# Local attention with a routed expert layer: two experts picked from batch 0's counts, three rounds written in line

## Chip, cores and metric

The kernel runs on one core of one Trainium2 chip. The metric is the device time of one execution in microseconds; lower is better. The five engines have their own instruction queues: TensorE (PE, with its weight loads as PEld), VectorE (DVE), ScalarE (ACT), GpSimd (POOL) and SyncE (SP, which here only issues DMAs and reads registers).

## Reference

Two parts follow one another. The first is attention over 2 batches, 8 heads, 768 positions and a head dimension of 64: each query sees the keys nearer than 16 positions, and besides them one key and one value for each block of 32 positions (the maximum of the block's keys, the mean of its values). The second part takes the result as 1536 rows of 512 numbers. Each row goes to the one of 8 experts whose logit is largest; an expert takes its first 384 rows and drops the others.

```python
k_sum = k.reshape(B, H, nb, block, D).max(axis=3)
v_sum = v.reshape(B, H, nb, block, D).mean(axis=3)
scores_l = np.where(np.abs(pos[:, None] - pos[None, :]) < 16, scale * (q @ k.T), -1e9)
scores_s = scale * (q @ k_sum.T) + np.log(block)
a = softmax(np.concatenate([scores_l, scores_s], axis=-1))
x = (a @ np.concatenate([v, v_sum], axis=2))      # 1536 rows of 512

logits = x @ w_gate                               # 8 experts
expert_idx = np.argmax(logits, axis=1)
gate_w = softmax(logits)[rows, expert_idx]
# the first 384 rows of each expert, in order, are disp[e]
h = np.maximum(np.einsum('ecd,edf->ecf', disp, w1), 0.0)   # F = 1024
y = np.einsum('ecf,efd->ecd', h, w2)
out[i] = gate_w[i] * y[expert_idx[i], pos[i]]              # 0 for dropped rows
```

The routing depends on the data. With these inputs batch 0 sends 363 rows to expert 0 and 405 to expert 7, and none to the others; both batches together send 504 to expert 0, 594 to expert 3 and 438 to expert 7. So three experts are in use, each is full, and expert 7 is full from batch 0 alone.

## The kernel before

**One order.** All work up to the end of the first expert round is a list of named steps, `SEQ`, which is run from left to right when the kernel is built. Each step appends its instructions to the queues of the engines that it uses, and each engine takes its queue in order. So a step's place in the list decides what stands ahead of it on its engine.

**Attention.** A chunk `c` (0 to 7) is two heads of one batch, a group `n` (0 to 23) four tiles of 64 queries. `k`, `q`, `t` and `v` load a chunk; `w`, `Q`, `kb`, `kp` and `vb`, `vt`, `vk`, `vp`, `vP` lay out keys, queries, block keys and block values. `kb` and `vb` are reductions on VectorE. Per group, `S` computes the scores (TensorE), `M` their maximum (VectorE), `E` the exponentials (ScalarE), `R` transposes them (TensorE), `K` copies them out of PSUM (ScalarE). `V` multiplies with the values (TensorE) and `N`, two steps on VectorE, divides by the sums; `V` of half `h` uses one PSUM buffer, which `N` of the half before sets free. Chunk 0 is prepared ahead of the list.

**Routing.** For each batch `x`, `X`, `l`, `L`, `g` compute the logits, `ch` and `ga` choose the expert and the gate's weight, and `ga` ends with a store of the batch's 768 rows to HBM (`xrow`). `pf` counts, `pl` places each row, and a census (`tk`) turns this by small matmuls into a table of row numbers by expert. `ts1` adds the tables of both batches (the tile `tid`).

**Rounds.** A round handles one expert with at most 384 rows. It loads w1 and w2 in four parts each (`lw`, `lW`) on SP's queue, gathers three tiles of 128 rows by indirect DMA (`fr`, POOL), transposes them (`T`, TensorE), and splits rows and weights into a high and a low part of fewer mantissa bits: `H` and `h1`, `h2` on ScalarE, `I` and `s1`, `s2` on VectorE. `u` is one eighth of the first layer (12 matmuls), `r` and `e` its relu and the low part of that; `D` is the second layer for one tile of rows (24 matmuls), after which the tile is weighted (tile `y`, ScalarE) and put to its rows in `out` by an indirect DMA on POOL.

Round 0 is picked from batch 0 alone: `pick` takes the expert with the most rows there, `first` reads its number into a register of SP, and its steps up to its first down tile (`D0`) stand in `SEQ`, between the routing steps of batch 1. The chain `rd` (the function `rounds`) then sorts the experts that are left by count, on VectorE. After the list the number of rounds left (`nr`) is read on all engines and the eight expert numbers on SP, and `tower` nests the other rounds in branches: within `If(nr > r)` the next round's loads and splits are interleaved with the down tiles of the round before; the `Else` finishes the last round.

Of the kernel before, what the change touches and what calls it, by code (L numbers as in the profile page):

```python
# [22 lines left out]
P = 128  # L23
# [89 lines left out]
q1 k1 S0 q3 z2 k2 M0 S1 t0 Q11a E0 M1 Q10p R0 kb1 E1 w1p q2 S2 K0 R1 kp1p k3 Q31a M2 Q30p v0 K1 S3 E2 kb2 w2p t1 R2 M3 S4 K2 vb0 kp2p E3 z3 R3 t3 M4  # L113
Q21a v1 vt0 S5 vk0 Q20p E4 kb3 R4 vp0 K3 M5 S6 vP0 E5 R5 w3p M6 E6 S7 kp3p vb1 misc zr V00 t2 M7 K4 v2 V01 N00 E7 N00 vt1 N01 q6 S8 N01 vk1 vb3 K5 vP1
S9 M8 t4 vp1 k4 R6 M9 E8 v3 R7 V10 K6 q4 vb2 K7 V11 k5 E9 N10 t5 N10 vt2 N11 S10 vk2 N11 vp2 vt3 vP2 S11 M10 vk3 Q61a vP3 R8 M11 E10 R9 vb4 V20 vp3 K8
Q60p K9 V21 N20 N20 E11 w4p q5 vt4 kb4 R10 t7 vk4 R11 K10 N21 v6 V30 N21 kp4p K11 v7 V31 N30 N30 x0 N31 k6 N31 Q40p Q41a x1 x2 X0a k7 X1a S12 w5p kb5
v5 X2a S13 M12 kp5p q7 vb5 E12 v4 vP4 l00 M13 t6 vp4 Q51a R12 E13 vt5 Q50p S14 vb7 vk5 R13 K12 vP5 M14 S15 L00a K13 vp5 E14 x3 M15 x4 X3a x5 X4a S16
X5a E15 g00 M16 R14 R15 E16 w6p kb6 S17 K14 K15 kp6p l01 kb7 w7p R16 L01a M17 S18 E17 kp7p g01 M18 R17 ch0 S19 E18 ch0 Q70p ch0 ch0 ch0 Q71a ch0 ch0
S20 M19 ch0 ga0 E19 ga0 pf0 ga0 pick ga0 M20 V40 pl0 K16 pick V41 pl0 pick vb6 K17 S21 pick pl0 pick pl0 pick pl0 pl0 pick pl0 vt6 pick R18 pl0 vk6
E20 R19 vP6 vt7 pl0 pl0 pl0 pl0 tk0 vk7 pick pick pick pick first lw0 lw1 M21 vp6 K18 S22 lw2 pads ts0 rows vP7 E21 N40 rows rows lw3 pads N40 R20  # L120
# [9 lines left out]
def attention_moe(ctx: ExitStack, tc: tile.TileContext, qT, kT, vT, vw, wg, w1, w2, cf, cm, cr, cv, out, cap: int):  # L130
# [121 lines left out]
    def key_blocks_put(c, eng):  # L252
        cast(eng, kt[c][:, :, WIN:KW], ksum[c].unsqueeze(1).to_broadcast([P, NT, NB]))
# [260 lines left out]
    class Round:  # L514
        def __init__(self, e, turn):
            self.e, self.turned, self.xp, self.hp, self.yp = e, turn, {}, {}, {}
# [114 lines left out]
        def down(self, j, tag=None):  # L631
            ps = psum.tile([P, DM], F32, tag=tag or f"av{j % 2}", name="yp", bufs=1)
            n = 0
            for f in range(KF):
                g, i = divmod(f, 2)
                for a, w in ((0, 0), (0, 1), (1, 0)):
                    nc.tensor.matmul(ps, self.h[g][:, i, a, P * j : P * j + P], self.w2[g][:, w, i, :], start=n == 0, stop=n == 3 * KF - 1)  # L637
                    n += 1
            self.yp[j] = ps

        def put(self, j):
            oid = small.tile([P, 1], I32, tag="oid", name="oid")
# [44 lines left out]
    sel, plans, ops = {}, [], {}  # L687
    ENGINES = {"p": nc.gpsimd, "a": nc.scalar, "v": nc.vector}
# [31 lines left out]
    def pick():  # L720
# [20 lines left out]
    def rows():  # L741
        sel["ids0"] = yield from places(tbs[0], sel["eq0"], 0, 1, "a")

    def rows_fetch(j):
        sel["R"].fetch_rows(sel["ids0"][:, 0], P * EARLY, j)

    def pads():
        eq0 = sel["eq0"][:, 0]
        mine = const.tile([P, E], F32, name="mine")
        c0 = const.tile([P, 1], F32, name="c0")  # L750
        nc.vector.tensor_tensor(out=mine, in0=sel["cl0"], in1=eq0, op=ALU.mult)
        yield
        nc.vector.tensor_reduce(out=c0, in_=mine, op=ALU.add, axis=AX.X)
        if nsub > 1:
            yield
            nc.vector.tensor_scalar(out=c0, in0=c0, scalar1=float(RW), scalar2=None, op0=ALU.min)
        sel["c0"] = c0
        yield
        pad = yield from padding(c0, 1, "a")
        sel["R"].pad = pad[:, 0]  # L760

    def rounds(s):
# [17 lines left out]
        cnt, k7, ei = yield from unpack(mx, E, f"b{s}")  # L780
# [50 lines left out]
    for r, R in enumerate(routes):  # L831
        for i in range(TPB):
            op(f"x{TPB * r + i}", R.turn, i)
            op_on(f"X{TPB * r + i}", R.take, i)
        for j in range(TPB // LB):
            op(f"l{r}{j}", R.logits, j)
            op_on(f"L{r}{j}", R.logits_keep, j)
            op(f"g{r}{j}", R.gather, j)
        chain(f"ch{r}", R.choose)
        op(f"pf{r}", R.prefix)  # L840
        chain(f"pl{r}", R.place)
        chain(f"ga{r}", R.gate)
# [119 lines left out]
```

## Time and profile before

| | |
|---|---|
| runs, us | 205.19, 207.51, 207.7; median 207.51 |
| profiled execution, us | 204.78 |
| its span, first to last instruction, us | 202.8 |
| mean granted TensorE clock | 0.967 of full speed |
| TensorE busy, us | 181.4 (89% of the span) |
| VectorE, ScalarE, GpSimd busy, us | 103.1, 103.1, 60.3 |
| DMA | 38.8 MB, mean 191 GB/s |

The span is the stretch that the trace covers; the profiled execution's own time is 2 us longer. All rows below are from this one execution, with times in us from the span's start. A granted clock of 1.00 is 2.4 GHz, one of 0.50 is 1.2 GHz. Attention ends at about 75 us, and the first round's products begin at 81.5.

### The profile page before, as it was taken

What the parts mean: (1) busy time and instruction counts of PE and PEld (TensorE: products, weight loads), DVE (VectorE), ACT (ScalarE), POOL (GpSimd) and SP (SyncE); (2) the same over time, 40 slices, a digit from 0 to 9 for tenths busy, and PEclk for the clock granted to TensorE, in tenths of its full rate; (3) what the DMA queues carried; (4) which work ended last, traced back from release to release, by engine and by line L of the source; (5) the groups of instructions that cost most, each with busy time, mean ns of one, the idle gap of its engine ahead of it and who ended that gap; (6) DMA issues with size and microseconds to landing.
All of it is one profiled execution on the core that took longest, in us unless ns stands there. A gap on an engine that the chain in (4) does not pass through costs nothing.

```text
span 202.8 us, 3980 instructions
## 1 busy us (share of the span) xinstructions
PE 181.4 (89%) x1461; PEld 159.5 (79%) x1461; DVE 103.1 (51%) x219; ACT 103.1 (51%) x227; POOL 60.3 (30%) x79
## 2 busy tenths in 40 slices
PE   7689999999996797999999349999998999989990
PEld 2577999989995595999988247999986899978870
DVE  3275697665599499836630760185470318520000
ACT  5568788789775699822101550473543146311100
POOL 6596638955416500000041020481012010000111
PEclk9889999999999999999999967999999999999996
DMA  6889599999858999803519999179001110000111
GB/s 201 273 294 324 112 319 320 363 269 265 200 205 252 360 383 403 325 2 117 199 52 300 360 377 352 68 236 366 21 0 52 52 53 5 2 10 3 52 55 52
DMA packets 20218, 38.80 MB, mean 191 GB/s; under 512 B 1450, under 2 KB 8284, under 8 KB 20188
## 3 DMA queue, kind: packets, MB, share of 16 engines
q1 hardware_dynamic: 18256, 33.43, 50.6%
q0 software_dynamic: 1440, 4.73, 6.6%
q10 hardware_dynamic: 492, 0.28, 0.7%
q8 instruction: 14, 0.23, 0.5%
q14 instruction: 16, 0.13, 0.2%
HBM read 29.77 MB, written 8.66 MB: 189 GB/s over the span
## 4 chain that ended last, share of the span: by engine, by line
PE 61%; DMA 10%; ACT 9%; issue 8%; DVE 7%; SPq 3%; POOL 1%; another core or an unknown queue 0%; POOLq 0%; DVEq 0%; ACTq 0%
PE hp L620 24%; PE yp L637 12%; PE sc L280 8%; PE pt L294 5%; PE av L308 5%; DMA w1r<-w 4%; DMA out<-y,oid 3%; DMA qc<-qT 2%; ACT prob L289 2%; PE xp L341 2%; ACT pts L298 2%; ACT w1h L227 1%; PE sc L281 1%; PE xgp L594 1%; PE lq L352 1%
## 5 line engine op out<-in xcount | busy, mean ns | idle before, releaser
L637 PE MATMUL yp<-w,h 128*128 128x512 f32 x216 | 52.4, 403 | 0.5 <-ACT h L625 0.5
L637 PEld LDWEIGHTS yp<-w,h 128*128 128x128 f32 x216 | 41.9, 196 | 9.6 <-issue 0.8
L620 PE MATMUL hp<-xh,w1h 128*128 128x384 f32 x96 | 32.7, 340 | 0.0
L620 PE MATMUL hp<-xh,w1l 128*128 128x384 f32 x96 | 32.2, 335 | 0.0
L620 PE MATMUL hp<-xl,w1h 128*128 128x384 f32 x96 | 32.1, 335 | 0.0
L646 POOL DMA_INDIRECT out<-y,oid x9 | 8.9, 994 | 76.9 <-ACT y L645 55.8
L289 ACT ACTIVATE prob<-sc,nm 128x120 f32<-128x120 f32 x96 | 27.0, 381 | 6.6 <-DVE nm L285 5.5
L280 PE MATMUL sc<-k,qb 128*128 128x120 f32 x192 | 26.9, 285 | 2.0 <-POOL qb L223 1.8
L280 PEld LDWEIGHTS sc<-k,qb 128*128 128x128 f32 x192 | 24.6, 200 | 3.6 <-POOL qb L223 2.1
L625 ACT ACTIVATE h<-hp 128x384 fp32r<-128x384 f32 x24 | 11.8, 492 | 29.6 <-PE hp L620 29.6
L285 DVE TENSOR_REDUCE nm<-sc 128x4 f32<-128x480 f32 x24 | 15.7, 656 | 17.6 <-PE sc L281 10.7
L629 DVE SCALAR_TENSOR_TENSOR h<-hp,h 128x384 fp32r<-128x384 f32 x24 | 13.3, 556 | 21.9 <-ACT h L625 21.8
L645 ACT ACTIVATE y<-yp,xgb 128x512 f32<-128x512 f32 x9 | 6.1, 687 | 33.2 <-PE yp L637 31.9
L575 DVE TENSOR_TENSOR w1l<-w1r,w1h 128x1024 fp32r<-128x1024 f32 x12 | 14.3, 1221 | 10.0 <-ACT w1h L227 10.0
L566 POOL DMA_INDIRECT xgb<-xrow,b0ids x6 | 8.6, 1426 | 35.5 <-DVE b0pad L494 34.0
L223 POOL TENSOR_SCALAR v<-vrow 25x520 f32<-25x520 f32 (+1 forms) x16 | 14.0, 874 | 15.8 <-ACT vrow L263 11.3
L620 PEld LDWEIGHTS hp<-xh,w1h 128*128 128x128 f32 x96 | 18.0, 188 | 0.3 <-issue 0.2
L620 PEld LDWEIGHTS hp<-xl,w1h 128*128 128x128 f32 x96 | 18.0, 188 | 0.1
L620 PEld LDWEIGHTS hp<-xh,w1l 128*128 128x128 f32 x96 | 18.0, 188 | 0.0
L227 ACT CAST w1h<-w1r 128x1024 fp32r<-128x1024 f32 x12 | 12.3, 1062 | 10.7 <-DMA w1r<-w 10.7
L294 PE MATMUL pt<-cft,prob 128*121 128x128 f32 x96 | 16.5, 301 | 0.9 <-ACT prob L289 0.7
L581 DVE TENSOR_TENSOR w<-w2r,w 128x1024 fp32r<-128x1024 f32 x12 | 14.6, 1226 | 3.9 <-ACT w L227 3.7
(116 smaller groups left out, 231.3 us busy)
## 6 DMA issues: line engine op xcount, KB each, us to landing
w1r<-w SPq DMA_DIRECT2D x12, 512.0 KB, 7.3
w2r<-w SPq DMA_DIRECT2D x12, 512.0 KB, 9.3
v<-vw SPq DMA_DIRECT2D x16, 292.5 KB, 7.2
kc<-kT SPq DMA_DIRECT2D x8, 400.0 KB, 6.1
xrow<-x SPq DMA_DIRECT2D x2, 1542.0 KB
vc<-vT SPq DMA_DIRECT2D x8, 384.0 KB, 4.6
out<-zrow SPq DMA_DIRECT2D x1, 3072.0 KB
qc<-qT SPq DMA_DIRECT2D x7, 384.0 KB, 7.0
```

Source lines behind the costliest of these rows:

```text
L223: eng.tensor_scalar(out=dst, in0=src, scalar1=f, scalar2=0.0, op0=ALU.mult, op1=ALU.add)
L227: nc.scalar.copy(out, in_)
L280: nc.tensor.matmul(self.sc[:, i, :], qb[c % NQ][:, t, :], kt[c][:, t, :], start=i == 0, stop=False)
L285: nc.vector.tensor_reduce(out=self.nm, in_=self.sc, op=ALU.max, axis=AX.X, negate=True)
L289: nc.scalar.activation(self.pr[:, i, :KW], self.sc[:, i], AF.Exp, bias=self.nm[:, i : i + 1])
L294: nc.tensor.transpose(self.pt[:KV, P * i : P * i + P], self.pr[:, i], ident)
L575: eng.tensor_tensor(out=self.w1l[g], in0=self.w1r[g], in1=self.w1h[g].bitcast(F32), op=ALU.subtract)
L581: eng.tensor_tensor(out=self.w2[g][:, 1], in0=self.w2r[g], in1=self.w2[g][:, 0].bitcast(F32), op=ALU.subtract)
L620: nc.tensor.matmul(ps, a[g][:, kk, fo : fo + P], x[:, kk, :], start=n == 0, stop=n == 3 * KD - 1)
L625: nc.scalar.activation(self.h[f // 2][:, f % 2, 0], self.hp[f], AF.Relu)
L629: nc.vector.scalar_tensor_tensor(out=h[:, f % 2, 1], in0=self.hp[f], scalar=0.0, in1=h[:, f % 2, 0].bitcast(F32), op0=ALU.max, op1=ALU.sub ...
L637: nc.tensor.matmul(ps, self.h[g][:, i, a, P * j : P * j + P], self.w2[g][:, w, i, :], start=n == 0, stop=n == 3 * KF - 1)
```

## The change

`pick` now takes the two experts with the most rows in batch 0. The first is round A, as before. The second is round B: its expert number is read from the same result (`firstB`), its rows and count come from the tables of both batches (`rowsB`, `padsB`). `rounds` removes both from the counts and sorts the others; the first of these is round C (`firstC`, `set`). All three rounds stand in `SEQ`, from loads to puts, without a branch; `down`, the row numbers of the output (`o`), the weighting (`y`) and the put (`P`) are steps of their own. `nr` is still read on all engines, and what is left after three rounds is done by a nest of branches at the end, a round at a time. `SEQ` is a new list throughout: the steps of attention and routing are the same but stand in another order. Ahead of the list, chunk 0's queries and block keys are laid out by other engines in other pieces.

The end of the list of before, from the last steps of the attention on:

```
h11a N61 K22 V70 s11v K23 V71 lW0 lW1 lW2 lW3 fill h12a N70 N70 x6 h13a s12v x7 X6a x8 s13v X7a X8a T0 N71 T1 N71 H0 l10 H1 I0 h20a I1 T2 L10a s20v H2
x9 h21a x10 I2 g10 X9a u0 s21v X10a h22a h23a s22v x11 u1 X11a s23v r0 e0 r1 l11 e1 u2 L11a g11 r2 u3 ch1 e2 ch1 ch1 ch1 ch1 ch1 ch1 u4 r3 ch1 e3 ga1
ga1 ga1 ga1 pf1 r4 cl1 u5 pl1 pl1 pl1 pl1 pl1 pl1 e4 pl1 pl1 u6 r5 pl1 pl1 pl1 pl1 e5 tk1 r6 u7 ts1 rd e6 rd rd rd rd rd rd r7 rd rd rd rd e7 D0 rd rd
rd rd rd rd rd rd rd rd rd rd rd
```

The diff, cut (of the new list the start, the stretch around pick, and the end):

```diff
@@ -110,19 +110,24 @@
+q1 k1 t0 S0 k2 z2 t2 S1 M0 q2 Q11a M1 Q10p E0 w1p q3 kb1 E1 S2 kp1p vb0 R0 z3 R1 M2 t1 K0 S3 K1 k3 kb2 E2 v0 w2p vt0 M3 v2 vk0 vb2 S4 kp2p E3 vP0 v1
...
+ch0 ch0 ch0 R17 ch0 ch0 M19 S20 ch0 ga0 E19 ga0 ga0 pf0 ga0 pick vt7 M20 V40 vk7 pick pl0 K16 pl0 vP7 pick V41 N40 pl0 K17 N40 S21 N41 pick vp7 N41
+pick pl0 pl0 pl0 R18 pick pl0 pl0 E20 R19 V50 pl0 pl0 pl0 pl0 K18 pick M21 V51 K19 N50 pick N50 E21 tk0 S22 N51 pick pick pick pick first N51 lw0 ts0
...
+u4 r3 ch1 e3 ga1 ga1 ga1 ga1 pf1 r4 cl1 lwB0 u5 pl1 pl1 pl1 lwB1 pl1 e4 pl1 pl1 pl1 pl1 u6 r5 pl1 pl1 pl1 pl1 padsB e5 padsB padsB padsB padsB padsB
+padsB tk1 r6 u7 ts1 rd e6 rd rowsB rd rowsB frB0 lwB2 rd rd rd rd rd r7 rd rd rd e7 D0 rd rd frB1 rd rd hB10a rd rd rd rd rd rd rd rd rd set firstC
+frB2 lwB3 lWB0 lWB1 lWB2 sB10v lWB3 hB11a nr lwC0 sB11v y0 frC0 lwC1 TB0 hB12a D1 HB0 sB12v P0 lwC2 IB0 hB13a sB13v lwC3 TB1 y1 frC1 TB2 HB1 D2 HB2
+IB1 IB2 P1 hB20a sB20v hB21a lWC0 sB21v hB22a lWC1 sB22v uB0 hB23a lWC2 sB23v TC0 rB0 lWC3 uB1 y2 eB0 oB0 frC2 uB2 rB1 P2 hC10a eB1 sC10v rB2 uB3 eB2
+oB1 TC1 rB3 uB4 hC11a eB3 sC11v uB5 rB4 eB4 rB5 uB6 hC12a eB5 sC12v uB7 rB6 oB2 eB6 rB7 HC0 eB7 DB0 HC1 IC0 hC13a IC1 sC13v TC2 yB0 PB0 DB1 HC2 IC2
+oC0 DB2 yB1 PB1 hC20a sC20v hC21a sC21v hC22a oC1 sC22v uC0 hC23a yB2 PB2 sC23v uC1 rC0 eC0 rC1 uC2 eC1 oC2 uC3 rC2 eC2 rC3 uC4 eC3 uC5 rC4 eC4 rC5
+uC6 eC5 uC7 rC6 eC6 rC7 eC7 DC0 DC1 yC0 PC0 DC2 yC1 PC1 yC2 PC2
...
-        def down(self, j, tag=None):
-            ps = psum.tile([P, DM], F32, tag=tag or f"av{j % 2}", name="yp", bufs=1)
+        def down(self, j):
+            ps = psum.tile([P, DM], F32, tag=("x", "av0", "av1")[j], name="yp", bufs=1)
...
+        def place(self, j):
+            self.oid[j] = small.tile([P, 1], I32, tag="oid", name="oid", bufs=3)
+            nc.vector.tensor_tensor(out=self.oid[j], in0=self.xg[:, j, DM : DM + 1], in1=self.pad[:, j : j + 1], op=ALU.add)
+
+        def weigh(self, j):
+            self.y[j] = work.tile([P, DM], F32, tag="y", name="y", bufs=2)
+            nc.scalar.activation(self.y[j], self.yp[j], AF.Copy, scale=self.xg[:, j, DM + 1 : DM + 2])
+
         def put(self, j):
...
     windows(0, nc.scalar, 0, 4)
     key_blocks(0)
-    key_blocks_put(0, nc.vector)
-    queries(0, 0, nc.vector, 0, 4)
+    queries(0, 0, nc.gpsimd, 0, 4)
     queries(0, 1, nc.scalar, 0, 4)
+    key_blocks_put(0, nc.vector, 0, 4)
+    key_blocks_put(0, nc.vector, 4, NT)
     windows(0, nc.scalar, 4, NT)
-    queries(0, 0, nc.gpsimd, 4, NT)
-    queries(0, 1, nc.gpsimd, 4, NT)
+    queries(0, 0, nc.vector, 4, 8)
+    queries(0, 1, nc.scalar, 4, 8)
+    queries(0, 0, nc.gpsimd, 8, NT)
+    queries(0, 1, nc.gpsimd, 8, NT)
...
-        top = const.tile([P, 1], F32, name="top0")
-        nc.vector.tensor_reduce(out=top, in_=key, op=ALU.max, axis=AX.X)
+        top = const.tile([P, E], F32, name="top0")
+        nc.vector.max(top, key)
         yield
-        _, k7, ei = yield from unpack(top, 1, "a")
+        _, k7, ei = yield from unpack(top[:, :2], 2, "a")
...
+    def begin(i):
+        (R[i].e,) = fetch(sel["ei0"][0:1, i : i + 1] if i < 2 else sel["next"][0:1, 0:1], E - 1)
...
+            yield
+            nc.vector.tensor_tensor(out=done, in0=done, in1=sel["eq0"][:, 1], op=ALU.add)
+            yield
...
+    def count():
+        sel["nr"] = fetch(plans[0][0][0:1, 0:1], E, ALL)[0]
...
-    nr = fetch(nai[0:1, 0:1], E, ALL)[0]
-    ev = fetch(ei[0:1, 0:E], E - 1)
...
-    tower(0, R0)
...
-            for r in range(E):
+            for r in range(1 if s == 0 else 0, E):
                 nest.enter_context(tc.If(nr > r))
```

## Rows read from the trace of the kernel before

**Rows 1.** The page: busy time by engine (share, instructions); a DMA with median to landing.

```profile
PE 181.4 (89%) x1461; PEld 159.5 (79%) x1461; DVE 103.1 (51%) x219; ACT 103.1 (51%) x227; POOL 60.3 (30%) x79
...
w1r<-w SPq DMA_DIRECT2D x12, 512.0 KB, 7.3
```

**Rows 2.** Busy time by stretch: engines (instructions), granted clock, DMA share, GB/s.

```profile
23.00:40.00 17.00, 17.00 (x280) 15.84 (x279) 13.55 (x27) 14.48 (x40) 10.73 (x17) 1.00 0.97 303
53.40:65.00 11.60, 9.76 (x131) 8.77 (x132) 11.10 (x42) 7.63 (x24) 4.69 (x5) 1.00 0.64 201
...
102.00:120.00 18.00, 12.00 (x59) 9.93 (x57) 7.79 (x13) 6.31 (x8) 4.02 (x4) 0.94 0.83 273
120.00:128.00 8.00, 8.00 (x28) 6.49 (x27) 0.85 (x2) 0.66 (x2) 1.00 (x1) 0.71 0.92 305
```

**Rows 3.** TensorE's timeline at the first crossing: start, us, instruction, idle before, releaser.

```profile
101.23 11.09 PE L637 MATMUL yp<-w,h 128*128 128x512 f32 x48
...
119.19 1.12 PE L594 MATMUL xgp<-cft,xgb 128*128 128x128 f32 x4 [6.00 <-DVE xl L602]
```

**Rows 4.** Chain of waits: start, us, what.

```profile
99.22 0.18 DVE tid L804
...
101.62 0.16 DVE nai L787
...
107.64 8.06 DMA w1r<-w
...
120.31 7.53 PE yp L637 x24
...
158.11 5.49 PE yp L637 x24
163.60 16.68 PE hp L620 x96
```

**Rows 5.** Busy time by stretch: two short stretches.

```profile
10.00:12.00 2.00, 2.00 (x11) 1.95 (x10) 0.96 (x2) 0.44 (x3) 1.92 (x4) 0.50 0.96 329
...
122.00:124.00 2.00, 2.00 (x7) 1.52 (x6) 0.00 (x0) 0.00 (x0) 0.00 (x0) 0.50 1.13 364
```

**Rows 6.** TensorE's timeline at the second and third crossings.

```profile
157.46 0.65 PE L594 MATMUL xgp<-cft,xgb 128*128 128x128 f32 x4 [1.16 <-DVE xl L602]
...
180.80 16.59 PE L637 MATMUL yp<-w,h 128*128 128x512 f32 x72 [0.53 <-ACT h L625]
```

**Rows 7.** SyncE's timeline: the store of batch 1's rows.

```profile
93.96 0.37 SPq L434 DMA_DIRECT2D xrow<-x  x1
```

**Rows 8.** Lines L652 (register loads) and L889 (branches): ns min/median/max, starts.

```profile
L652 DVEq TENSOR_LOAD <-nai x1: 541/541/541, 103.4 to 103.4; - x1
...
L889 PEldq COMPARE_BRANCH  x4: 65/196/3292, 103.2 to 193.2; - x4
...
L889 POOLq COMPARE_BRANCH  x4: 34/44/53, 102.4 to 198.9; - x4
```

**Rows 9.** Busy time by stretch: between the store and the next loads.

```profile
101.00:103.00 2.00, 2.00 (x11) 1.70 (x10) 1.83 (x9) 0.49 (x1) 0.00 (x0) 1.00 0.00 0
```

**Rows 10.** The tile xgb (gathered rows): its DMAs.

```profile
DMA to landing us min/median/max: 4.4/6.5/7.7
```

**Rows 11.** Timelines of TensorE, GpSimd and ScalarE at the start.

```profile
8.62 2.06 PE L280 MATMUL sc<-k,qb 128*128 128x120 f32 x8 [1.81 <-POOL qb L223]
...
7.28 1.29 POOL L223 TENSOR_SCALAR qb<-qc 64x512 f32<-64x512 f32 x2 [3.47 <-DMA qc<-qT]
...
11.73 1.12 ACT L289 ACTIVATE prob<-sc,nm 128x120 f32<-128x120 f32 x4 [1.56 <-DVE nm L285]
```

**Rows 12.** TensorE's timeline around the first census; VectorE's group of value reductions.

```profile
61.80 0.64 PE L450 MATMUL bank<-colm,rowm 128*128 128x24 bf16 x12 [1.11 <-DVE colm L421]
...
64.83 0.92 PE L308 MATMUL av<-v,pts 121*64 121x65 f32 x24 [0.68 <-DVE x L319]
...
L257 DVE TENSOR_REDUCE vsq<-vc 128x24 f32<-128x768 f32 x8 | 7.5, 943 | 0.4 <-PE bank L260 0.4
```

More of the change, by code (lines that the diff above doesn't have):

```diff
@@ L117 @@
[L117 to L120, printed above, removed]
@@ L779, in rounds @@
         yield
-        cnt, k7, ei = yield from unpack(mx, E, f"b{s}")
+        cnt, k7, ei = yield from unpack(mx, E, f"r{s}")
+        if s == 0:
+            sel["next"] = ei
         yield
@@ L830, in attention_moe @@
         op(f"z{i}", zero_q, nc.gpsimd, i)
-    for r, R in enumerate(routes):
+    for r, rt in enumerate(routes):
         for i in range(TPB):
-            op(f"x{TPB * r + i}", R.turn, i)
-            op_on(f"X{TPB * r + i}", R.take, i)
+            op(f"x{TPB * r + i}", rt.turn, i)
+            op_on(f"X{TPB * r + i}", rt.take, i)
         for j in range(TPB // LB):
[L836 to L842, printed above, removed]
@@ L843, in attention_moe @@
-    for name, f in dict(misc=misc, zr=zeros, fill=fill, first=first, tk0=census, tk1=last_census, ts0=first_tokens, ts1=all_tokens, cl1=last_clip).items():
+            op(f"l{r}{j}", rt.logits, j)
+            op_on(f"L{r}{j}", rt.logits_keep, j)
+            op(f"g{r}{j}", rt.gather, j)
+        chain(f"ch{r}", rt.choose)
+        op(f"pf{r}", rt.prefix)
+        chain(f"pl{r}", rt.place)
+        chain(f"ga{r}", rt.gate)
+    for name, f in dict(misc=misc, zr=zeros, fill=fill, nr=count, set=settle, tk0=census, tk1=last_census, ts0=first_tokens, ts1=all_tokens, cl1=last_clip).items():
@@ L859, in attention_moe, with on_round @@
-    for j in range(RT):
-        op(f"fr{j}", rows_fetch, j)
-        on_first(f"T{j}", "turn", j)
-        on_first(f"H{j}", "turn_high", j)
-        on_first(f"I{j}", "turn_low", j)
-    for f in range(KF):
-        on_first(f"u{f}", "products", f)
-        on_first(f"r{f}", "relu", f)
-        on_first(f"e{f}", "rest", f)
-    on_first("D0", "down", 0, "x")
+    def on_round(i, name, f, *a):
+        op(name, lambda: getattr(R[i], f)(*a))
+    for i, c in enumerate(["", "B", "C"]):
+        op(f"first{c}", begin, i)
+        if i < 2:
+            chain(f"rows{c}", lambda i=i: rows(i))
+            chain(f"pads{c}", lambda i=i: pads(i))
+        for g in range(4):
+            on_round(i, f"lw{c}{g}", "load_w1", (g,))
+            on_round(i, f"lW{c}{g}", "load_w2", (g,))
+            for e, eng in ENGINES.items():
+                on_round(i, f"h{c}1{g}{e}", "high_w1", g, eng)
+                on_round(i, f"s{c}1{g}{e}", "low_w1", g, eng)
+                on_round(i, f"h{c}2{g}{e}", "high_w2", g, eng)
+                on_round(i, f"s{c}2{g}{e}", "low_w2", g, eng)
+        for j in range(RT):
+            op(f"fr{c}{j}", rows_fetch, i, j)
+            on_round(i, f"T{c}{j}", "turn", j)
+            on_round(i, f"H{c}{j}", "turn_high", j)
+            on_round(i, f"I{c}{j}", "turn_low", j)
+            on_round(i, f"D{c}{j}", "down", j)
+            on_round(i, f"o{c}{j}", "place", j)
+            on_round(i, f"y{c}{j}", "weigh", j)
+            on_round(i, f"P{c}{j}", "put", j)
+        for f in range(KF):
+            on_round(i, f"u{c}{f}", "products", f)
+            on_round(i, f"r{c}{f}", "relu", f)
+            on_round(i, f"e{c}{f}", "rest", f)
@@ L930, in attention_moe @@
                 for g in range(4):
-                    R.split_w1(g)
-                    R.split_w2(g)
+                    more.split_w1(g)
+                    more.split_w2(g)
                 for j in range(RT):
-                    R.turns(j)
+                    more.turns(j)
                 for f in range(KF):
-                    R.up(f)
-                finish(R, 0)
+                    more.up(f)
+                for j in range(RT):
+                    more.down(j)
+                    more.place(j)
+                    more.weigh(j)
+                    more.put(j)
```

137 lines of the change are left out of this document (45 added, 92 removed).

## The prediction

> **What bounds the kernel now.** I read the busy shares first: TensorE is busy 181.4 us of a span of 202.8 us, 89%, and no other computing engine more than 51% [rows 1]. So the span is TensorE's work plus the holes in it, and for a change of order the question is which holes it closes. The table of busy time by stretch says where to look: in 23 to 40 TensorE has no hole, in 53.4 to 65 it has 1.8 us, in 102 to 120 6.0 us, and in 120 to 128 none, but there the granted clock is 0.71 [rows 2]. Then I read TensorE's own timeline at the crossings between the three rounds. From the first round's last product on it runs 48 down products without a hole (101.23 to 112.3), then the transposes of two tiles, and then it waits 6.00 us for DVE's xl [rows 3]. The chain of waits says why: the expert of the next round is known only with the plan's last numbers (101.62); after register work on SP the first layer's weights are on their way for 8.06 us, until 115.7 [rows 4]; ScalarE casts them in order, and the copy of the rows (xh) stands behind the casts. The third transpose needs the PSUM buffer that this copy and xl set free. After the hole the clock is at 0.50, the 1.2 GHz level [rows 5], and the 24 down products that follow take 7.53 us, where the 24 of the second crossing take 5.49 us [rows 4]. The second crossing has the same hole in small, 1.16 us, since the weights were there already, and at the third 0.53 us are lost [rows 6].
>
> **The first crossing, A to B.** After the change the expert of round B comes from batch 0's counts, with A's. The loads of w1's first three parts stand on SP behind the store of batch 1's rows (issued at 93.96, [rows 7]) and not behind a register load at 102. Their buffers are emptied by A's own splits, long before. w1's last part and the four parts of w2 stand behind firstC on SP, the register load of round C's expert, which waits for the plan's sort on DVE; that ended by 101.6 [rows 4], and DVE has some four small steps more ahead of it, 0.2 us each (tid to nai are 12 steps in 2.4 us, [rows 4]). With a register load of 0.5 us [rows 8] these parts start at about 103.5, and with the 7.3 us to landing of a part of w1 [rows 1] the last is there by 111 and w2 some 3 to 5 us later. Down tiles and transposes cover that: TensorE's order becomes D0, TB0, D1, TB1, TB2, D2, uB0. Its work there is 72 down products, 16.59 us in the last round's row, and 12 transposes, 0.65 us for 4 in a row of now, so at most 1.9 [rows 6]; uB0 starts at 101.2 + 18.5 = 119.7, where D2 now ends at 120.31 + 7.53 = 127.84 [rows 4]. What I count is what the rows name: the hole of 6.00 us and the slow clock's 7.53 - 5.49 = 2.04 us, together -8.0 us.
>
> What is late next is the gather of round B's rows. TB0 stands ahead of D1 in TensorE's order, so D1 and everything behind it waits if the rows are not there when D0 ends, at 101.23 + 16.59/3 = 106.8. The row numbers need the sum of the two batches' tables (tid, 99.22, [rows 4]) and then six DVE steps, one of them the rest of a tile of h: about 1.4 us at the pace above, so 100.7. The batch's own store, which the gather must follow, has drained by then (no traffic in 101 to 103, [rows 9]). A gather takes 4.4 to 7.7 us to land, at the median 6.5 [rows 10]: 105.1, 107.2 or 108.4. So TB0 waits 0 to 1.6 us; I take the median, +0.5 us. The hole of 1.81 us at the start was followed by a clock of 0.50 in 10 to 12 [rows 5, 11], those of 1.11 and 0.68 us in 53.4 to 65 were not [rows 2, 12]; so the upper end carries 2.0 us more, the price above: 0 to +3.6 us.
>
> **The second crossing, B to C**, becomes the same order with everything loaded: TC0 and TC1 stand inside B's products, the third between the down tiles. -1.2 us, the hole. The buffer for C's rows is A's; its gathers follow A's three outputs, some 40 us ahead of HC0. The splits of C's w1 run under B's products, as the splits of w2 do now; its w2 splits stand behind B's down tiles and reach into uC0, as two score-sized buffers allow.
>
> **The third, and the tail.** At 180.80 TensorE waited 0.53 us for h at the entry of the else branch [rows 6]; in line the first down products need only the first tiles of h. -0.5 us (0 to -0.5). After the last product, which ends at 197.4 [rows 6], come y, its put and its landing until 202.8; all stay. Every engine now reads the count of rounds left (nr) between D0 and TB0; such a load took 0.54 us on DVE [rows 8], and TensorE, which had one too, ran through without a hole [rows 3]: nothing, or +0.5 us if it stands bare. One branch is left at the end, over a body of seven rounds. The four compare-and-branches on TensorE's load queue took 65 to 3292 ns, at the median 196; those on GpSimd, which ends the kernel, at most 53 ns [rows 8]. Beside the landing of the last put I take it at nothing; bounds 0 and +3.3 us.
>
> The Trainium skill speaks against that branch: Runtime: NRT & Kernel Launch, section Instruction fetch mechanics, says that a taken branch to a target outside the window of fetched instructions waits for the fetch. The one of 3292 ns agrees with it, those on GpSimd do not show it; by the rule the end could come up to 3.3 us later.
>
> **The start.** Now the second group's scores wait 1.81 us for GpSimd, which makes both heads of tiles 4 to 11 in 1.29 us from 7.28 on; the exponentials E1 begin at 11.73 after a wait of 1.56 us for their maximum [rows 11]. The change gives tiles 4 to 7 to DVE and ScalarE, a head each: half the work of one of GpSimd's two, side by side, so about 0.35 us and scores from 7.6 on. Then M1 is done about when E0 ends (11.73 - 1.56 = 10.2), and E1 follows. -1.5 us at most; I take -1.3 (0 to -1.8).
>
> **The order of attention.** In 53.4 to 65 DVE is busy 11.1 of 11.6 us [rows 2], and TensorE's holes are one of 1.11 us ahead of the first census (for colm) and one of 0.68 us ahead of V50, for the normalisation that frees its buffer [rows 12]. The new order puts N40 and N41 between the steps of pick, so V50 and V51 fill TensorE ahead of the census, and it moves two reductions (vb6, vb7: 0.94 us each, [rows 12]) out of the stretch. Against that, the four N steps now stand ahead of the first expert's choice and so of its loads; the two roughly cancel for the choice. I take half of the 1.8 us, -0.9, and as bounds -1.8 and +3.0 (a hole like these at each of four places more), since nearly every name has moved.
>
> **The sum**: -8.0 + 0.5 - 1.2 - 0.5 - 1.3 - 0.9 = -11.4 us. The profiled execution took 204.78 us, 2.0 us more than its span; so 193.4 us on that scale. The runs' median is 207.51 us, 1.3% above it, and their lowest is 205.19: the same ratio gives 196.0 from the median, 193.8 from the lowest. I forecast 195 us.
>
> **The rivals.**
> - *The gather becomes the wait* (12%). The place is TB0; it decides if the rows land 1.5 us or more after D0. For it: w1 is on the DMA engines at the same time, and landings reach 7.7 us [rows 10]. Against: the median leaves 0.5 us. It gives the upper end, 193.4 + 3.1 = 196.5, about 199 on the median's scale.
> - *The branch at the end stalls* (5%), as TensorE's slowest did [rows 8]: +3.3 us, 196.7, or 199 to 200.
> - *Within 2%* (8%): the gather's wait, the upper end of the attention's order and no gain at the start come together, 3.1 + 3.9 + 1.3 = +8.3 us: 201.7, 204 on the median's scale.
> - *Slower: the attention stage pays* (4%). DVE takes its queue in order, and 16 reductions (vb at 0.94 us [rows 12], and as many kb over as many columns) stand among 24 score maxima. If the new places put each just ahead of a maximum for which ScalarE and then TensorE wait, 16 x 0.94 = 15 us are lost, and with the gains of start and attention gone it is 193.4 + 15 + 2.2 = 210.6, 213 on the median's scale. From 10 of the 16 on the gain is gone. Against: the same reductions stand there today, and TensorE has no hole in 23 to 40 [rows 2].
> - *It isn't three rounds* (1%). If the second pick had no rows, or four experts were in use, a round would be left for the loop at the end, which nothing overlaps: 7.3 us of loads [rows 1], 16.7 us of products [rows 4], 16.6 us more [rows 6] and about 5 us of tail are 45 us, so 240 us. The routing of these inputs speaks against it: batch 0 uses experts 7 and 0 only, both batches 0, 3 and 7.
>
> **Chances and range.** The forecast, from 191 (start and attention at their better ends) to 199, gets the other 70%. Faster by over 2%, about what a measurement of this kernel tells from no change, means under 203.4: the forecast and the first two rivals, 0.87; within 2% 0.08; slower 0.05. For 8 in 10 I take 191 to 200.
>
> **What would show it.** In the new profile TensorE's timeline should run from round A's last product to the end of the last down tile with no hole but one under 1.6 us at TB0; the granted clock should be 1.00 from there to the end; w1's loads for round B should issue from about 94, not 105; the second scores should start before 8.0. I would be wrong if the hole at TB0 were over 2 us with a clock of 0.50 after it, if TensorE had new holes in the attention stage, or if the span went on much more than 5.4 us after the last product.

## The result and the profile after

The changed kernel takes 196.41 us (median of 4 runs, 196.18 to 197.3), where the kernel before, run beside it, takes 206.35 us (4 runs, 204.16 to 207.7): a ratio of 0.960 with a 95% interval of 0.954 to 0.967. In the experiments below some executions are slower as a whole by 1.5% or more; the medians count them, the ratios leave them out. The forecast of 195 us lies 1.4 us below, and the range holds the time. The profiled execution took 196.38 us with a span of 194.4, so 8.4 us less than before on both scales, where the sum of the prediction said 11.4.

The page's line of busy times answers to [rows 1]:

```profile
PE 175.4 (90%) x1461; PEld 155.8 (80%) x1461; DVE 102.5 (53%) x227; ACT 105.0 (54%) x228; POOL 58.2 (30%) x80
```

TensorE runs the same 1461 instructions in 6.0 us less busy time; the other 2.4 us are idle time that is gone. The mean granted clock is 0.995, before 0.967. 2.0 of the 6.0 us are the down products (50.4 us for all 216, before 52.4), those behind the hole of 6.00 us, which no longer run at the lower clock. How much of the rest is the clock and how much the attention's new order isn't shown.

TensorE's timeline from round A's first down product on (start, us, instruction, idle before with its releaser), which answers to [rows 3, 6]:

```profile
99.69 5.64 PE L642 MATMUL yp<-w,h 128*128 128x512 f32 x24
107.61 0.66 PE L599 MATMUL xgp<-cft,xgb 128*128 128x128 f32 x4 [2.28 <-DMA xgb<-xrow,bids]
108.03 5.72 PE L642 MATMUL yp<-w,h 128*128 128x512 f32 x24
113.59 1.03 PE L599 MATMUL xgp<-cft,xgb 128*128 128x128 f32 x8
114.38 5.70 PE L642 MATMUL yp<-w,h 128*128 128x512 f32 x24
...
119.92 0.33 PE L625 MATMUL hp<-xh,w1h 128*128 128x384 f32 x1
...
171.03 16.52 PE L642 MATMUL yp<-w,h 128*128 128x512 f32 x72
```

Read it from the brackets: from 99.69 to the last product's end at 187.55 there is one hole, 2.28 us at TB0, for the gathered rows of round B (xgb). The 6.00, 1.16 and 0.53 us of before are gone, and the 24 products behind the hole take 5.72 us. Those behind the hole of 6.00 us took 7.88 in the same view (7.53 in the chain of waits, where the row starts later):

```profile
119.96 7.88 PE L637 MATMUL yp<-w,h 128*128 128x512 f32 x24
```

The start, from the timelines of TensorE and ScalarE, answers to [rows 11]:

```profile
7.19 1.15 PE L285 MATMUL sc<-k,qb 128*128 128x120 f32 x8 [0.68 <-DVE vsq L694]
...
8.56 2.12 ACT L294 ACTIVATE prob<-sc,nm 128x120 f32<-128x120 f32 x8
```

The second scores begin at 7.19 (8.62 before), and the exponentials of both groups, E0 and E1, run back to back from 8.56 to 10.68, where E1 alone went from 11.73 on.

Busy time by stretch (engines with instructions, granted clock, DMA share, GB/s), as in [rows 2]:

```profile
23.00:40.00 17.00, 15.66 (x234) 14.64 (x234) 10.79 (x23) 13.83 (x40) 8.00 (x11) 1.00 1.04 304
53.40:65.00 11.60, 11.34 (x180) 10.78 (x180) 10.30 (x47) 7.31 (x25) 3.02 (x4) 1.00 0.58 183
...
120.00:128.00 8.00, 8.00 (x49) 7.97 (x48) 5.29 (x8) 4.05 (x6) 2.05 (x2) 1.00 1.02 375
```

The stretch from 53.4 has 0.3 us of holes, where it had 1.8. The one from 23 to 40, full before, has 1.3 us of them, and in 120 to 128 the clock is 1.00 instead of 0.71.

The gain by place, from the two profiles:

| stretch | before, us | after, us | change | forecast |
|---|---|---|---|---|
| up to round A's first down product (D0) | 101.23 | 99.69 | -1.5 | -2.2 |
| from there to round B's first product of u | 26.44 | 20.23 | -6.2 | -7.5 |
| from there to round C's first down product | 53.13 | 51.11 | -2.0 | -1.7 |
| round C's down products | 16.59 | 16.52 | -0.1 | 0 |
| last product's end to the end of the span | 5.41 | 6.85 | +1.4 | 0 |

(The starts are 101.23, 127.67 and 180.80 before, 99.69, 119.92 and 171.03 after.) The first crossing gave 1.3 us less than forecast, and the end of the kernel took 1.4 us back; the start and the attention gave 0.7 us less in this execution. The experiments ask where the gather's 2.3 us come from, what the end costs, and which part of the change brings the rest.

### The profile page after: what moved, and what is told of

The parts are those of the page before. It is cut to its first block, busy times and chain, and to the rows that moved or that the text cites. A ratio compares the mean times of both kernels' runs of the same rounds, so it can differ in the third digit from the quotient of the medians.

```text
span 194.4 us, 3977 instructions
## 1 busy us (share of the span) xinstructions
PE 175.4 (90%) x1461; PEld 155.8 (80%) x1461; DVE 102.5 (53%) x227; ACT 105.0 (54%) x228; POOL 58.2 (30%) x80
## 4 chain that ended last, share of the span: by engine, by line
issue 28%; PE 27%; DMA 25%; ACT 7%; DVE 5%; POOL 4%; SPq 1%; POOLq 0%; ACTq 0%
DMA out<-y,oid 11%; PE hp L625 9%; DMA kc<-kT 5%; PE sc L285 5%; DMA xgb<-xrow,aids 4%; PE yp L642 4%; DMA xgb<-xrow,bids 3%; ACT prob L294 3%; DMA qc<-qT 2%; PE pt L299 2%; PE xp L346 2%; PE av L313 1%; PE lq L357 1%; PE xgp L599 1%; DVE x L324 1%
## 5 line engine op out<-in xcount | busy, mean ns | idle before, releaser
L642 PE MATMUL yp<-w,h 128*128 128x512 f32 x216 | 50.4, 391 | 0.0
L642 PEld LDWEIGHTS yp<-w,h 128*128 128x128 f32 x216 | 40.3, 188 | 8.2
L285 PEld LDWEIGHTS sc<-k,qb 128*128 128x128 f32 x192 | 23.3, 191 | 6.6 <-POOL qb L228 1.9
L655 POOL DMA_INDIRECT out<-y,oid x9 | 9.7, 1081 | 58.4 <-ACT y L652 57.5
L652 ACT ACTIVATE y<-yp,xgb 128x512 f32<-128x512 f32 x9 | 6.2, 686 | 27.7 <-PE yp L642 18.2
L228 POOL TENSOR_SCALAR v<-vrow 25x1040 f32<-25x1040 f32 (+1 forms) x16 | 13.4, 840 | 9.9 <-ACT vrow L268 9.0
L303 ACT COPY pts<-pt 121x512 f32<-121x512 f32 x24 | 13.8, 594 | 4.7 <-PE pt L299 3.9
L313 PE MATMUL av<-v,pts 121*64 121x65 f32 x384 | 13.8, 224 | 2.4 <-DMA v<-vw 1.2
L313 PEld LDWEIGHTS av<-v,pts 121*64 121x64 f32 x384 | 12.4, 137 | 4.1 <-issue 3.0
```

The costliest lines, as they stand in the source:

```text
L228: eng.tensor_scalar(out=dst, in0=src, scalar1=f, scalar2=0.0, op0=ALU.mult, op1=ALU.add)
L285: nc.tensor.matmul(self.sc[:, i, :], qb[c % NQ][:, t, :], kt[c][:, t, :], start=i == 0, stop=False)
L303: nc.scalar.copy(self.pts[:KV], self.pt[:KV])
L313: nc.tensor.matmul(av[c, h][o : o + QT, ip, hh, :], G[3 * c + t // 4].pts[:KV, P * i + QT * hh : P * i + QT * hh + QT], vt[c][:KV, t, hh, ...
```

## The experiments

Times are medians, ratios are to the kernel before on the same chip. The first group ran beside a kernel before of 204.88 us, the second (e2b, e4, e5, e6) beside 204.79, the third (e8, e10) beside 203.47. "D0 to DC0" is the stretch from round A's first down product to round C's, 79.57 us before and 71.34 after: it leaves out the attention and the end.

### The changed kernel again

> The changed kernel itself, once more, on the same chip as the runs beside it: 196.4 us as in its first runs, with the hole of 2.3 us at TB0 and 6.8 us between the last product and the end of the span.

195.51 us (193.88 to 197.09), 0.954 (0.949 to 0.960). D0 starts at 97.18, D0 to DC0 is 70.92 us, the hole at TB0 1.87, and the span ends 7.28 us after the last product (191.9 less 184.62). So the rounds repeat within half a microsecond, and the start of D0 doesn't: 2.5 us lie between these two profiles of one kernel. In this one TensorE is busy 17.00 us of 17 in 23 to 40.

### e1: the end without the nest of branches

```diff
-            for r in range(1 if s == 0 else 0, E):
-                nest.enter_context(tc.If(nr > r))
...
-                    more.put(j)
```

> Leaves out the loop for rounds beyond the third (never entered with these inputs) and with it the last branch; nr is still read. Theory: the branch and the join behind it cost the 1.4 us by which the stretch after the last product has grown (5.4 to 6.8 us): 1.2 to 1.6 us less than the changed kernel, that stretch 5.4 us or shorter. Rival: the stretch is the landing of the last put: no difference (under 0.4 us).

194.67 us, 0.948 (0.943 to 0.954): 1.2 us less than the changed kernel by the ratios, but the intervals overlap, so the time alone doesn't settle it. The profiles do. GpSimd's timeline at the end of e1:

```profile
188.51 0.98 POOL L655 DMA_INDIRECT out<-y,oid  x1 [4.46 <-ACT y L652]
```

and of the changed kernel:

```profile
188.60 0.98 POOL L655 DMA_INDIRECT out<-y,oid  x1 [4.46 <-ACT y L652]
```

The instructions of the branches' line there (duration in ns: min, median, max; then the first and last start):

```profile
L915 POOLq EVENT_SEMAPHORE  x4: 17/42/2288, 188.9 to 189.1; - x4
...
L915 PEldq COMPARE_BRANCH  x1: 4098/4098/4098, 183.3 to 183.3; - x1
...
L915 POOLq COMPARE_BRANCH  x1: 53/53/53, 188.4 to 188.4; - x1
...
L915 POOLq INC_SWDGE_SEM  x1: 548/548/548, 191.4 to 191.4; - x1
```

The last puts start 0.09 us apart, and both kernels move its rows in the same microsecond. Traffic of both, the changed kernel's first (columns as in the table of busy time by stretch):

```profile
190.00:191.00 1.00, 0.00 (x0) 0.00 (x0) 0.00 (x0) 0.00 (x0) 0.00 (x0) 1.00 0.70 270
191.00:192.00 1.00, 0.00 (x0) 0.00 (x0) 0.00 (x0) 0.00 (x0) 0.00 (x0) 1.00 0.00 0
```

```profile
190.00:191.00 1.00, 0.00 (x0) 0.00 (x0) 0.00 (x0) 0.00 (x0) 0.00 (x0) 1.00 0.67 262
```

Then e1 ends at 192.9 and the changed kernel at 194.4. Without the nest the end takes 192.9 - 187.46 = 5.44 us, as before the change (5.41); with it 6.85 and 7.28. The price of the nest is 1.4 to 1.8 us, and the rows show where it lies. Behind the branch GpSimd waits 2.29 us on a semaphore; by the time that the wait is over, at 191.4, the last put's rows have been moved. Only then comes a step of 0.55 us on the DMA semaphores, and only at 192.0 GpSimd's drain with which the program closes. In e1 this drain starts right behind the put and runs while its rows are moved (the changed kernel's first):

```profile
L956 POOLq DRAIN  x3: 45/107/1549, 192.0 to 194.1; - x3
```

```profile
L931 POOLq DRAIN  x3: 40/113/3767, 188.3 to 192.6; - x3
```

The longest of the three is the first in both, so it is over at 193.6 with the nest and at 192.1 without; from there to the end both take 0.8 us. In the kernel before, the wait and the step are:

```profile
L889 POOLq EVENT_SEMAPHORE  x2: 43/43/43, 198.2 to 198.3; - x2
L889 POOLq INC_SWDGE_SEM  x1: 535/535/535, 198.4 to 198.4; - x1
```

There they are over by 198.9, while the last put (198.44 to 199.42) is still being issued, and wait for nothing; the closing drain starts at 199.1. TensorE's own compare-and-branch in the changed kernel took 4.10 us, but from 183.3 on, under the last products.

### e2 and e2b: batch 1's store with the DMA engines to itself

```diff
-... cl1 lwB0 u5 pl1 pl1 pl1 lwB1 pl1 e4 ... frB0 lwB2 rd ... set firstC frB2 lwB3 lWB0 ...
+... cl1 u5 pl1 pl1 pl1 pl1 e4 ... frB0 rd ... set firstC lwB0 lwB1 lwB2 lwB3 hB10a frB2 lWB0 ...
```

This is e2b. e2 moved only lwB0 and lwB1; its third part still ran beside the store, and the first split of round B's weights (hB10a) then stood ahead of their load, so that the high part of that quarter came from round A's expert.

> The first two w1 loads of round B (lwB0, lwB1) are moved behind firstC in the list, so that the store of batch 1's rows has the DMA engines for itself. Theory: these loads share the engines with the store and hold back the gather, which must follow it; then the gather of round B starts at about 98.9 and not 101.15, the hole at TB0 goes from 2.3 to under 0.5 us, and the run is about 2 us shorter than the changed kernel. Rival: the start of the gather waits for DVE (nai, 100.9), as the profile's releaser says: gather still at 101, no gain, and w1 lands later.

194.95 us, 0.947 (0.940 to 0.954), an interval that overlaps the changed kernel's; D0 to DC0 71.03 us, the same as with the loads early, so the 2 us expected are not there in the rounds. The hole at TB0 is gone, and one of 1.90 us for DVE's xl stands at the third transposes. For the reasons above it isn't a clean test.

> All four w1 loads of round B, and the first cast of them, are moved behind firstC, so that nothing shares the DMA engines with the store of batch 1's rows; everything is computed as in the changed kernel. Theory (the loads hold back the store, the gather follows the store): the gather starts as soon as its row numbers exist, 0.9 us ahead of D0's start and not 1.2 to 1.5 us after it, and TB0 waits for nothing; w1 lands later, ScalarE's casts hold back xh, and the third transpose waits about 2 us for its buffer: so the time is that of the changed kernel within 0.7 us. Rival (the gather starts late for DVE's or GpSimd's own reasons): it starts 1 us or more after D0 as before, and the run is 1 to 2 us slower than the changed kernel.

195.35 us, 0.959 (0.948 to 0.969); D0 to DC0 70.65 us. The timeline of e2b, GpSimd's gather of round B among TensorE's rows:

```profile
98.98 1.00 POOL L571 DMA_INDIRECT xgb<-xrow,bids  x1 [31.29 <-DVE r0ci L468]
99.08 5.65 PE L642 MATMUL yp<-w,h 128*128 128x512 f32 x24
104.57 0.60 PE L599 MATMUL xgp<-cft,xgb 128*128 128x128 f32 x4
...
112.62 0.66 PE L599 MATMUL xgp<-cft,xgb 128*128 128x128 f32 x4 [1.51 <-DVE xl L607]
```

The gather now starts 0.1 us before D0. In the changed kernel it starts 1.5 us after D0; its store, the loads beside it, the row numbers and the gather are these rows of the timeline:

```profile
92.43 0.37 SPq L439 DMA_DIRECT2D xrow<-x  x1
93.04 8.35 SPq L562 DMA_DIRECT2D w1r<-w  x4
98.67 0.18 DVE L492 TENSOR_REDUCE bids<-bpk 128x3 int32<-128x24 f32 x1
101.15 1.00 POOL L571 DMA_INDIRECT xgb<-xrow,bids  x1 [31.75 <-DVE nai L806]
```

The row numbers are ready at 98.85, and the gather starts 2.3 us later. The releaser that its row names is whichever DVE step ended last (nai here, r0eq in e3, r0ci in e2b), none of which makes its numbers; what it still needs is the store. It starts 8.7 us after its store was issued, and 8.4 to 8.9 us after it in four more profiles in which w1 is loaded beside the store (the changed kernel again, e1, e3, e8); in e2, with less of w1 beside the store, it is 7.77 us, and in e2b 7.15. In e2b the traffic beside the store is down to 37 GB/s in 97 to 98, 5.2 us after its issue at 91.83; in the changed kernel 97 to 99 has 144 and 196 GB/s with the engines busy all the time. So the early loads hold the store back, and the gather with it. Without them the wait moves to the casts of w1 (1.51 us for xl at the third transposes), and nothing is won or lost: D0 to DC0 is 70.65 us, against 71.34 and 70.92.

### e3: something to do for TensorE until the rows are there

The second down tile is cut into halves of 12 products, and TB0 stands between them.

```diff
-        def down(self, j):
+        def down(self, j, part=None):
...
-            for f in range(KF):
+            for f in range(KF) if part is None else range(KF // 2 * part, KF // 2 * (part + 1)):
...
-... lwC1 TB0 hB12a D1 HB0 ...
+... lwC1 hB12a D1< TB0 D1> HB0 ...
```

> D1 is cut in two halves of 12 products and TB0 stands between them, so TensorE has 2.7 us of work while the rows land; loads stay. Theory: the hole at TB0 was the only cost of the late rows: 2.3 us shorter than the changed kernel, no hole over 0.3 us from D0 to the end. Rival: the later TB0 only moves the wait to xl of TB0 (the third transpose's buffer) or to uB0: gain under 1 us.

192.50 us (192.12 to 193.13), 0.939 (0.934 to 0.943): about 3 us below the changed kernel (0.954) on the same chip, and the two intervals don't touch. Its timeline:

```profile
97.95 8.36 PE L643 MATMUL yp<-w,h 128*128 128x512 f32 x36
106.16 0.66 PE L599 MATMUL xgp<-cft,xgb 128*128 128x128 f32 x4
106.57 3.00 PE L643 MATMUL yp<-w,h 128*128 128x512 f32 x12
109.42 1.03 PE L599 MATMUL xgp<-cft,xgb 128*128 128x128 f32 x8
110.21 5.70 PE L643 MATMUL yp<-w,h 128*128 128x512 f32 x24
```

There is no hole, and D0 to DC0 is 68.92 us, 2.0 and 2.4 us less than in the changed kernel's two profiles, whose holes were 1.87 and 2.28. So this hole is worth about its own length.

### e4 and e5: the change in two

e4 takes start and order of before up to the first step ch1, with only the new steps (firstB, o0 to o2) put in, and the new rounds behind it. e5 takes the new start and order up to the same step, and the list, pick and branches of before behind it.

Both edits are of this kind, e4 from new to old as shown, against the changed kernel, and e5 from old to new, against the kernel before (the list's beginning and the queries of chunk 0):

```diff
-q1 k1 t0 S0 k2 z2 t2 S1 M0 q2 Q11a M1 Q10p E0 w1p q3 kb1 E1 S2 kp1p vb0 R0 z3 R1 M2 t1 K0 S3 K1 ...
+q1 k1 S0 q3 z2 k2 M0 S1 t0 Q11a E0 M1 Q10p R0 kb1 E1 w1p q2 S2 K0 R1 kp1p k3 Q31a M2 Q30p v0 K1 ...
...
-    queries(0, 0, nc.vector, 4, 8)
-    queries(0, 1, nc.scalar, 4, 8)
-    queries(0, 0, nc.gpsimd, 8, NT)
-    queries(0, 1, nc.gpsimd, 8, NT)
+    queries(0, 0, nc.gpsimd, 4, NT)
+    queries(0, 1, nc.gpsimd, 4, NT)
```

> The start and the order of steps of before up to the first step of batch 1's routing, the changed kernel from there on. Theory: start and attention's order are worth the 1.5 to 2 us by which D0 began earlier; so 1.0 to 2.5 us slower than the changed kernel, D0 at about 101, the rest from D0 on 71 us as in the changed kernel. Rival: the new order gains nothing (the holes it makes between 23 and 77 us eat the start): same time within 0.7 us.

197.56 us (196.53 to 199.72), 0.966 (0.956 to 0.975). From D0 on its profile is that of the changed kernel: D0 to DC0 is 71.25 us, with a hole of 2.21 us at TB0. D0 starts at 103.24 there, but the profiled execution is the longest of the four (199.72 us), so nothing is read from that.

> The new start and order up to batch 1's routing, then the old list and the nested branches for rounds B and C. Theory: the rounds in line are worth 6 to 7 us, so 201 to 203 us, 0.985 to 0.99 of the kernel before, with the 6 us hole and a clock of 0.50 back at the first crossing. Rival: the order of attention is what gained: 198 us or less.

201.27 us (200.37 to 202.54), 0.987 (0.976 to 0.998). The crossing of e5 is that of before in every row of TensorE's timeline:

```profile
97.47 11.09 PE L637 MATMUL yp<-w,h 128*128 128x512 f32 x48
...
115.71 1.11 PE L594 MATMUL xgp<-cft,xgb 128*128 128x128 f32 x4 [6.28 <-DVE xl L602]
116.47 7.10 PE L637 MATMUL yp<-w,h 128*128 128x512 f32 x24
```

D0 to DC0 is 79.42 us (before 79.57) and the end 5.43, so all that e5 gains lies ahead of D0. The parts add up, as closely as their intervals tell: the rounds alone are 1 - 0.966 = 3.4% (2.5 to 4.4), the start and the attention alone 1.3% (0.2 to 2.4), together 4.7%, and the whole change 4.6% by its run in the first group and 4.0% by its first runs.

### e6 and e10: three rounds in line, but the second expert from both batches

Only the first expert of pick is used, and rounds B and C come from the plan, whose loads and gathers stand behind its last step. e10 has TB0 between the halves of the second down tile besides.

```diff
-        (R[i].e,) = fetch(sel["ei0"][0:1, i : i + 1] if i < 2 else sel["next"][0:1, 0:1], E - 1)
+        (R[i].e,) = fetch(sel["ei0"][0:1, 0:1] if i == 0 else sel["next"][0:1, i - 1 : i], E - 1)
...
-... set firstC frB2 lwB3 lWB0 ...
+... firstB set lwB0 lwB1 lwB2 lwB3 frB0 frB1 frB2 firstC lWB0 ...
```

> Three rounds in line as in the changed kernel, but B and C are both taken from the plan over both batches (as before the change), so B's loads and gather are issued only when the plan exists. Theory: the order in line (TB0, TB1, TB2 between down tiles) already hides most; the early pick is worth the loads' lead only: the gather starts 3 to 4 us after D0, TB0 waits 3 to 5 us, 1 to 3 us slower than the changed kernel. Rival: the early pick is the whole gain: holes of 6 us or more and a slow clock again, 5 us or more slower.

199.46 us, 0.975 (0.965 to 0.985). D0 to DC0 is 73.95 us. TensorE's timeline, and the granted clock in its busy time by stretch:

```profile
109.24 0.66 PE L598 MATMUL xgp<-cft,xgb 128*128 128x128 f32 x4 [3.29 <-DMA xgb<-xrow,r0ids]
109.65 7.32 PE L641 MATMUL yp<-w,h 128*128 128x512 f32 x24
116.81 1.03 PE L598 MATMUL xgp<-cft,xgb 128*128 128x128 f32 x8
```

```profile
111.00:113.00 2.00, 2.00 (x7) 1.52 (x6) 1.76 (x2) 0.75 (x3) 0.62 (x1) 0.50 1.07 385
```

The hole is 3.29 us, and the 24 products behind it take 7.32 us, partly at the 1.2 GHz level. At the third transposes there is no wait for xl, although round B's w1 is loaded only from 101.96 on, 1.7 us behind D0's start (before 4.3 us behind it, in the changed kernel 6.7 us ahead): the 24 products of the second tile, which now stand behind TB0, cover the casts. They do so with the hole and the slow clock ahead of them; in e2b, with loads 1.4 us behind D0's start and no hole at TB0, the same order left 1.51 us of waiting for xl. So of the 8.2 us that the rounds gained (79.57 to 71.34), 5.6 come without the early choice, and 2.6 with it (3.3 against the shortest profile of the changed rounds, e1's 70.67).

> B and C from the plan over both batches, as in the late-expert run, with D1 in halves around TB0. Theory: the early pick buys only the lead of the rows; with 2.7 us of products ahead of TB0 the hole is under 1 us and the clock stays at 1.00: 69.5 to 70.5 us from D0 to round C's D0, so 1 us more than with the early pick, 193.5 to 196 us. Rival: with late loads the weights become the wait (uB0 or the third transpose): a hole of 2 us or more elsewhere, 197 us or more.

195.66 us (194.33 to 197.39), 0.962 (0.952 to 0.972); D0 to DC0 70.86 us:

```profile
98.39 8.36 PE L642 MATMUL yp<-w,h 128*128 128x512 f32 x36
108.00 0.66 PE L598 MATMUL xgp<-cft,xgb 128*128 128x128 f32 x4 [1.24 <-DMA xgb<-xrow,r0ids]
108.41 3.00 PE L642 MATMUL yp<-w,h 128*128 128x512 f32 x12
```

The hole at TB0 is 1.24 us, a little over the 1 us expected, and the products behind it run at full rate. With the split tile in both, the early choice is worth 70.86 - 68.92 = 1.9 us; and the split alone, with the old choice, makes the rounds as short as those of the change.

### e8: the split tile and no nest

e3 and e1 together.

> D1 in halves around TB0, and without the loop for rounds beyond the third (it leaves out that fallback, which these inputs never enter). Theory: the hole at TB0 and the join at the end are separate and add up: 1.2 to 1.6 us under the kernel with D1 in halves alone, about 191 us; 69 us from D0 to round C's D0, 5.4 us after the last product. Rival: without the hole the end is bound by the puts: less than 0.5 us from leaving out the loop.

191.86 us (190.88 to 193.1), 0.942 (0.936 to 0.948), the lowest time of all, though by its ratio not below e3 (0.939): the difference can't be told in the time. In the profile both effects stand side by side: D0 to DC0 68.92 us, as in e3, and from the last product at 185.89 to the end at 191.3 5.4 us, where e3 has 7.0 (183.39 to 190.4). e3 beats both kernels and keeps the nest for more than three experts.

## Why the prediction was right

**What bounds the kernel** held: from D0 on the time followed the holes in TensorE's order, and each that was named is gone.

**The first crossing** came true in its terms but one. Forecast -7.5 us with the gather's wait, measured -6.2. The terms for xl and the clock came true: no wait for xl, 24 products at full rate. The gather's wait was the mis-sized term: +0.5 forecast, 0 to 1.6 as its bounds; it was 2.28, 1.87 and 1.62 us in three profiles of this order, and 2.21 in e4's. The step that failed is "the batch's own store has drained by then", read from the row without traffic in 101 to 103 [rows 9]. That row belongs to a kernel in which nothing runs beside the store. The change itself issues round B's loads behind it, and the prediction moved these loads (from about 105 to 94) without asking whom they would share the DMA engines with there. Its own last condition, a hole of more than 2 us with a clock of 0.50 after it, was met by half: the hole was over 2 us in two of these four profiles, the clock stayed at 1.00 in all. Its other two conditions were met in part as well, new holes in the attention stage and a later end; both are taken up below. The 2.0 us added to the upper bound for the clock were not spent.

**The rival "the gather becomes the wait"** is thus what happened, as its place was TB0 and it was to decide at 1.5 us; its price of 3.1 us above the sum was 1.1 for the wait and 2.0 for the clock, and 1.8 and nothing were measured. Its ground (landings of 7.7 us beside w1's traffic) was a different one: the gathers landed in 5.9 to 8.0 us, but the first started 2.3 us after its row numbers were ready.

**The second and third crossing**: -1.7 forecast, -2.0 measured, no hole left in either. The third came true for another reason than the one given. The 0.53 us were not a wait for h, although the row names it, but TensorE's branch at the entry of the else branch. Of the kernel before:

```profile
L889 PEldq COMPARE_BRANCH  x1: 3292/3292/3292, 177.3 to 177.3; - x1
180.77 16.20 PEld L637 LDWEIGHTS yp<-w,h 128*128 128x128 f32 x72 [0.82 <-issue]
```

and of e5, which has the same branch:

```profile
L892 PEldq COMPARE_BRANCH  x1: 3595/3595/3595, 173.1 to 173.1; - x1
176.02 0.49 ACT L625 ACTIVATE h<-hp 128x384 fp32r<-128x384 f32 x1 [1.59 <-PE hp L620]
176.86 16.19 PEld L637 LDWEIGHTS yp<-w,h 128*128 128x128 f32 x72 [1.20 <-issue]
```

In both, TensorE loads its next weights 0.2 us after the branch is over (180.6 and 176.7). In e5 ScalarE's last h was done at 176.51, 0.35 us ahead of these weights, and the hole is 0.91 us, longer with the longer branch. So what made this hole was the slowest branch of [rows 8], which the prediction counted only as a risk for the end; the -0.5 us came true by luck.

**The tail** was taken at nothing, with bounds 0 and +3.3 us; it was +1.4 us, 1.4 to 1.8 by e1. The bound was taken from TensorE's compare-and-branch, which did stall again, for 4.10 us (3.4 to 4.1 in the other profiles with the nest), and cost nothing, as it lay under the last products. On GpSimd the branch took 53 ns as forecast. What cost was a step that the prediction didn't have: the engines come together behind the branch, and the closing drain starts only when GpSimd has waited there until the last put is through. In the kernel before the same instructions were done while the last put was being issued, and waited for nothing.

The Trainium skill's rule on the branch (Runtime: NRT & Kernel Launch, section Instruction fetch mechanics: a taken branch beyond the fetched window waits for the fetch) fits the 4.10 us on TensorE's load queue, and the 3.29 us that made the third crossing's hole; that it is a fetch for which TensorE waits there, no row shows. It isn't what delays the end, and the 53 ns on GpSimd don't show it.

**The start and the attention**, -2.2 forecast: -1.5 in the profile compared, and -2.35 as the mean of ten profiles with the new order, whose D0 starts from 97.18 to 100.45 (mean 98.88, against 101.23 in the one profile of before). e5 gives 1.3% of the time, 2.7 us. The start does what was said, with scores from 7.19 (said: 7.6) and E1 behind E0. That nearly all steps moved at no cost is not shown for each; the 1.3 us of holes in 23 to 40 are in this one profile, and 17.00 of 17 us are busy there in the nine others. From 40 to 53.4, where TensorE had no hole before, all ten have 0.25 to 0.6 us.

**In sum**, forecast -11.4, measured -8.4: the first crossing gave 1.3 less, the tail took 1.4, the start and the attention gave 0.7 less, the other crossings 0.3 more and the last products 0.1 more. That 195 is nearer to the measured time than the sum's own 193.4 is due to the scale (the runs' median of before stood above the profiled execution), not to the terms.

**What the prediction credited wrongly** is the choice of the expert. It put the gain of the first crossing down to weights that are loaded from 94 on. By e2b the early loads close the hole for xl (1.51 us without them) but bring nothing on the whole, as they cost as much at TB0. By e6 the order in line, with the second down tile behind TB0, brings 5.6 of the 8.2 us with loads that start behind D0; by e10 half a tile more of cover brings as much as the early choice. The early choice is worth 1.9 to 3.3 us.

## What to carry to other kernels

When a load is moved earlier, ask which transfer it will run beside: here the early weights slowed the store on which the next gather waited, and what one wait gave up the other took. A hole for data that is about 2 us late is closed by placing half a tile of independent products ahead of the instruction that waits, at no cost (it gained 2.0 to 2.4 us here), and this worked as well as knowing the expert earlier. A branch around work that isn't done still costs where the engines come together behind it, if that is at the very end (1.4 to 1.8 us), and where it stands between two stretches of TensorE's work (0.53 and 0.91 us). A row's releaser is the step that ended last, not always the one that was needed: the gather's and the third crossing's both named the wrong one.

## What was not expected of the hardware

Holes of 1.62 to 2.28 us on TensorE at TB0 were followed by products at full rate (5.70 to 5.72 us for 24), one of 3.29 us by 7.32 us, one of 6.28 us by 7.10 us and the one of 6.00 us by 7.88; the hole of 1.81 us at the start of the kernel before, followed by a clock of 0.50 [rows 5, 11], is shorter than two of those that were followed by full rate, so the length of a hole alone doesn't tell what follows it. The store of 768 rows takes 7.15 us or less from its issue to the gather that needs it when it runs alone, and 8.4 to 8.9 us beside the loads of w1 that SyncE issues behind it. TensorE's compare-and-branch takes 3.3 to 4.1 us where it passes over the bodies of rounds that aren't run, in every profile that has such a branch (ten of twelve); on ScalarE, VectorE and GpSimd it takes 50 to 72 ns.
